# A fused attention and GEGLU block on one core: side matmuls paced by columns per iteration with fillers, two head quads interleaved, one gelu instruction in the last feed-forward group

## The chip, the core and the metric

The kernel runs on one core of one Trainium2 chip. A core has five engines that follow their own instruction lists and wait for each other by semaphores: PE (matmuls, from SBUF into the accumulation memory PSUM), ACT (one function per element, here mostly exp), DVE (other elementwise work), POOL, and SP, which here only issues DMAs. [...]

The metric is the device time of one execution in microseconds (us): the median of three runs. A separate execution was profiled; its trace is what the text reads.

## What is computed

One transformer block on 2048 tokens of width 512, with 32 heads of width 16 and a hidden width of 1792. Six modulation vectors come from a conditioning vector c.

```
mod = (silu(c) @ w_mod).reshape(1, 6, 1, -1)
sa, ca, ga, sb, cb, gb = mod[:, 0..5]
h = layernorm(x) * (1 + ca) + sa
q, k, v = heads of h @ wqkv
p = softmax(q @ k.T * 16**-0.5);  o = p @ v
x = x + ga * (o @ wo)
h = layernorm(x) * (1 + cb) + sb
x = x + gb * ((gelu(h @ w_gate) * (h @ w_up)) @ w_down)
```

gelu is the tanh form. Weights and activations are bfloat16, sums are float32.

## The kernel before, in words

**Blocks.** Queries are taken in five groups (`GROUPS`): three of 512 tokens, two of 256. Within a group the heads are taken in eight quads of four heads (`qd`), and the keys in 128-token tiles. A "tile" of scores is one head's 128 keys by 512 query columns (or two such key tiles by 256), one PSUM bank. There are 2048 such tiles.

**The main loop** (`stream`) runs 683 iterations. Iteration c takes the next three tiles: `qk` issues their score matmuls on PE into three of six PSUM banks (`scp`, shown as `ps_sc`; two sets of three alternate), and ACT makes one exp of 128 x 1536 into the SBUF ring `E` of 24 slots. Then PE multiplies earlier exp results with the values (`pv_round`: four matmuls that run side by side, one per head of the quad, into the bank `pv`), always two iterations behind. A column of ones in the values gives the softmax denominators; at the end of a quad DVE copies the bank to `osb`, and the denominators are turned into reciprocals by way of DRAM (`fin1`, `fin2`, put off by 5 and 10 iterations).

**Order on PE.** PE runs its list in order. The score matmuls of iteration c+1 wait for the exp of iteration c-1, since they write its banks, and the exp of c+1 waits for them. Whatever else stands in PE's list between two score groups delays the next score group, and so may delay ACT.

**Side work.** Everything else goes through the eighth bank, `mi` (`ps_mi`): the projections of q, k, v (`proj_q`, `proj_k`, `proj_v`; 4 matmuls of 512 columns, or 16 of 128), transposes (8 of 128 columns), the output projection (`wo`: 8 matmuls of 512 per 128 tokens) and the feed-forward part of the group before (`G`, `U`: 4 matmuls each; `down`: 14 per 128 tokens). `first_side` and `group_side` return lists of such items. Each item issues all its matmuls at once and then the DVE instruction that empties `mi`; `stream` spreads the items evenly over the iterations through the table `sched`. So an iteration has either no side matmul, or a whole item of 1024, 2048, 4096 or 7168 columns.

**First stage.** The prologue loads inputs, computes layernorm of tokens 0 to 511, and projects k and q of the first quad pair. Keys of the other three token groups (512 tokens each) are made inside the loop: layernorm statistics (`ln_stat`) and normalization on DVE, transposes and modulation, then K and V. Quad 0 walks over all 16 key tiles first, so its fifth iteration or so already needs the second token group, and so on.

**Gelu.** In the loop, gelu is made from DVE products and an ACT Tanh, so that exp and tanh share ACT's function table. The last group's feed-forward part (`tail`) does the same with ACT Square and Copy, five DVE instructions per pair of chunks and a Tanh, in a four-stage software pipeline.

**Queues.** The first loads are issued by SP and ACT; all later DMAs by SP.

## Time and profile before

| what | value |
|---|---|
| time, median of 3 runs | 1115.35 us (1114.75 to 1116.24) |
| the profiled execution | 1115.72 us |
| its span, first to last instruction | 1114.0 us |
| first exp starts, last exp ends | 18.7 us, 1069.2 us |
| exp instructions in the loop | 683 |
| mean granted PE clock | 0.779 |

The span divides into three parts: up to the first exp (lead), from there to the end of the last exp (stream), and the rest (tail). In the views that follow, a row of the timeline gives start, duration, engine, operation, the tile written and those read, a count, and in brackets how long the engine stood idle before it and what ended that. A row of the windows gives a stretch, the busy time in it and the granted PE clock as a share of full speed.

### The profile page before, as it was taken

What the parts mean: (1) busy time and instruction counts of PE and PEld (TensorE: products, weight loads), DVE (VectorE), ACT (ScalarE), POOL (GpSimd) and SP (SyncE); (2) the same over time, 40 slices, a digit from 0 to 9 for tenths busy, and PEclk for the clock granted to TensorE, in tenths of its full rate; (3) what the DMA queues carried; (4) which work ended last, traced back from release to release, by engine and by line L of the source; (5) the groups of instructions that cost most, each with busy time, mean ns of one, the idle gap of its engine ahead of it and who ended that gap; (6) DMA issues with size and microseconds to landing.
All of it is one profiled execution on the core that took longest, in us unless ns stands there. A gap on an engine that the chain in (4) does not pass through costs nothing.

```text
span 1114.0 us, 15292 instructions
## 1 busy us (share of the span) xinstructions
PE 853.9 (77%) x6638; PEld 257.9 (23%) x6638; DVE 362.9 (33%) x796; ACT 967.4 (87%) x740; POOL 7.2 (1%) x13
## 2 busy tenths in 40 slices
PE   5677777777777777777778788788787878787757
PEld 2222222211121111112212111112222223222225
DVE  7732223121033222321123322231126552343346
ACT  2489999999979999998799999999888997999924
POOL 2000000000000000000000000000000000000000
PEclk7688888787577777777967767776969999668878
DMA  6000000520000000000000000000000000000000
GB/s 246 1 1 11 11 11 11 183 55 11 11 1 11 10 11 11 11 9 7 25 11 11 11 11 11 11 1 11 29 12 12 11 12 25 9 13 9 11 15 10
DMA packets 28621, 24.97 MB, mean 22 GB/s; under 512 B 14445, under 2 KB 22826, under 8 KB 28554
## 3 DMA queue, kind: packets, MB, share of 16 engines
q1 hardware_dynamic: 27226, 22.16, 6.8%
q10 hardware_dynamic: 1328, 1.84, 0.5%
q8 instruction: 52, 0.85, 0.3%
q14 instruction: 15, 0.12, 0.0%
HBM read 21.36 MB, written 2.61 MB: 22 GB/s over the span
## 4 chain that ended last, share of the span: by engine, by line
ACT 64%; PE 29%; DVE 6%; issue 1%; DMA 0%; DVEq 0%
ACT E L210 62%; PE ps_mi L201 16%; PE ps_sc L201 9%; PE ps_pv L201 3%; ACT wreg L210 2%; DVE st L243 1%; PE ps_mi L205 1%; DVE nwt L213 1%; DVE hreg L220 1%; DVE xw L213 0%; DVE mv L246 0%; DVE rstd L224 0%; DVE xs L213 0%; DMA xs<-in_A_x_dram 0%; DVE kme L220 0%
## 5 line engine op out<-in xcount | busy, mean ns | idle before, releaser
L210 ACT ACTIVATE E<-ps_sc 128x1536 bf16<-128x1536 f32 (+2 forms) x697 | 939.8, 1485 | 107.0 <-PE ps_sc L201 106.3
L201 PE MATMUL ps_sc<-qT,kme 32*128 32x512 bf16 (+1 forms) x1280 | 171.4, 419 | 108.2 <-ACT E L210 105.8
L201 PE MATMUL ps_pv<-E,vaug 128*17 128x512 bf16 (+1 forms) x2560 | 244.4, 409 | 5.2 <-DVE osb L227 3.9
L201 PE MATMUL ps_sc<-qT,kmo 32*128 32x512 bf16 (+1 forms) x1280 | 164.4, 401 | 102.9 <-ACT E L210 101.7
L201 PE MATMUL ps_mi<-wreg,mreg 128*128 128x512 bf16 (+1 forms) x448 | 142.2, 455 | 1.2 <-DVE wreg L227 0.9
L201 PEld LDWEIGHTS ps_sc<-qT,kme 32*128 32x128 bf16 x1280 | 37.6, 96 | 245.9 <-ACT E L210 219.7
L201 PEld LDWEIGHTS ps_sc<-qT,kmo 32*128 32x128 bf16 x1280 | 37.3, 94 | 233.0 <-ACT E L210 198.3
L201 PEld LDWEIGHTS ps_pv<-E,vaug 128*17 128x17 bf16 x2560 | 52.1, 89 | 164.2 <-issue 150.0
L227 DVE CAST wreg<-ps_mi 128x512 bf16<-128x512 f32 (+1 forms) x56 | 35.0, 625 | 165.5 <-PE ps_mi L201 165.5
L213 DVE TENSOR_TENSOR hreg<-ps_mi,wreg 128x512 bf16<-128x512 f32 (+1 forms) x56 | 34.9, 623 | 97.6 <-PE ps_mi L201 97.3
L201 PEld LDWEIGHTS ps_mi<-wreg,mreg 128*128 128x128 bf16 x448 | 40.7, 112 | 68.5 <-issue 49.3
L201 PE MATMUL ps_mi<-dreg,hreg 128*128 128x512 bf16 x210 | 54.0, 402 | 0.1
L213 DVE TENSOR_TENSOR wreg<-wreg 128x1024 bf16<-128x1024 bf16 (+1 forms) x84 | 52.5, 626 | 2.9
L227 DVE COPY osb<-ps_pv 128x512 f32<-128x512 f32 (+1 forms) x40 | 23.3, 582 | 76.8 <-PE ps_pv L201 76.6
L201 PE MATMUL ps_mi<-hreg,wreg 128*128 128x512 bf16 x120 | 44.8, 513 | 0.0
L213 DVE TENSOR_TENSOR onorm<-osb,rb 128x512 bf16<-128x512 f32 (+1 forms) x40 | 23.2, 580 | 52.8 <-DMA rb<-scr_rec 52.8
L201 PE MATMUL ps_mi<-wo,onorm 128*128 128x512 bf16 x112 | 36.1, 480 | 0.2 <-DVE xw L213 0.2
L213 DVE TENSOR_TENSOR xw<-ps_mi,gb 128x512 bf16<-128x512 f32 x15 | 10.4, 692 | 67.7 <-PE ps_mi L201 67.6
L220 DVE TENSOR_SCALAR wreg<-wreg 128x1024 bf16<-128x1024 bf16 (+1 forms) x56 | 21.9, 392 | 30.2 <-ACT wreg L210 29.3
L220 DVE TENSOR_SCALAR kmo<-ps_mi,rm 128x512 bf16<-128x512 f32 x15 | 11.3, 750 | 55.3 <-PE ps_mi L201 55.3
L210 ACT ACTIVATE wreg<-wreg 128x1024 bf16<-128x1024 bf16 (+1 forms) x28 | 28.5, 1018 | 0.0
L227 DVE CAST qT<-ps_mi 128x512 bf16<-128x512 f32 x15 | 10.4, 692 | 51.8 <-PE ps_mi L201 51.8
(94 smaller groups left out, 343.5 us busy)
## 6 DMA issues: line engine op xcount, KB each, us to landing
rb<-scr_rec SPq DMA_DIRECT2D x96, 64.0 KB, 2.0
mreg<-in_w_mod_dram SPq DMA_DIRECT2D x1, 2048.0 KB, 17.6
out_dram<-xs SPq DMA_DIRECT2D x16, 128.0 KB, 1.7
rb<-scr_rec SPq DMA_DIRECT2D x60, 32.0 KB, 1.8
mreg<-in_B_w_gate_dram SPq DMA_DIRECT2D x1, 1792.0 KB, 7.2
mreg<-in_B_w_up_dram SPq DMA_DIRECT2D x1, 1792.0 KB, 11.3
dreg<-in_B_w_down_dram SPq DMA_DIRECT2D x1, 1792.0 KB, 17.2
wreg<-in_A_wqkv_dram SPq DMA_DIRECT2D x1, 1536.0 KB, 10.6
```

The costliest lines, as they stand in the source:

```text
L201: return self.rec("pe", lambda e: e.matmul(out, lhsT, rhs, start=start, stop=stop, tile_position=tp), [lhsT, rhs], [out])
L205: return self.rec("pe", lambda e: e.transpose(out, in_, ident), [in_, ident], [out])
L210: return self.rec("act", lambda e: e.activation(out, in_, func, scale=scale, **kw), rd, [out])
L213: return self.rec(eng, lambda e: e.tensor_tensor(out, a, b, op), [a, b], [out])
L220: return self.rec(eng, lambda e: e.tensor_scalar(out, a, s1, s2, **kw), rd, [out])
L227: return self.rec(eng, lambda e: e.tensor_copy(out, in_), [in_], [out])
L243: return self.rec("dve", lambda e: e.bn_stats(out, in_), [in_], [out])
```

## The change

The diff has four parts.

**1. Side work as generators, paced.** `first_side` and `group_side` become generators (`side_first`, `side_k`, `side_v`, `side_q`, `side_mod`, `side_wo`, `side_ffn`) that yield before each piece of up to 512 columns, -1 (or -2, -4) where the next piece must wait for one (two, four) iterations because DVE has to empty `mi`, and 0 at the end. `plan` gives each generator a first and a last iteration; `pump` hands out columns per iteration so that the work left is spread over the iterations left. `require` runs a generator forward at once where a key or value tile is needed that isn't made yet. Where an iteration has under `FILL` = 1280 columns in all (counted with 128 for each score tile and 512 for each `pv_round`) and `mi` is free, `stream` adds filler matmuls into `mi` whose result nobody reads.

**2. First two quads interleaved.** The first 128 tiles go by token group: group 0 of quad 0 and quad 1, group 1 of both, and so on. Quad 1 accumulates in the sixth bank of `scp`, so these 140 tiles (128 and a run-out of 12) go in chunks of three and two in turn: 56 exps for 140 tiles, and 692 exps in all. `osb`, `rb` and their DRAM copies get two to four slots by size, and the 256-column groups use separate columns of `onorm` (`OCOL`), so that `wo` of one group may lie later.

**3. Prologue.** The first loads are ordered anew and `wqkv` comes in six pieces; silu of c is made in columns (`tcol`) from four one-column matmuls, before the statistics on DVE; statistics of token tiles 4 to 8 move to ACT (Copy and Square with accumulated sums, two instructions a tile); more warm-up matmuls stand between.

**4. Tail.** The denominators' selection matmul (`self32`) goes ahead of the `wo` matmuls; the feed-forward part uses one `Gelu_apprx_tanh` per pair of chunks on ACT, one DVE instruction for the product with `up`, and a two-stage order.

```diff
+FILL = 1280
+OCOL = (0, 0, 0, 0, 256)
...
+    def require(self, keys):
+        for key in keys:
+            while key not in self.have:
+                w = self.work[0]
+                w[4] = next(w[0], 0)
...
+    def side_proj(self, col, g, fin):
+        mi = self.mi[:, :]
+        for dci in range(NDC):
+            yield 512
+            self.mm(mi, self.wqkv[:, dci, col:col + P], self.hT[:, dci, 512 * g:512 * g + 512],
+                    start=(dci == 0), stop=(dci == NDC - 1))
+        fin(mi)
+        yield -1
...
+    def plan(self, gstart):
+        a = gstart[1]
+        w = [(self.side_first, 0, 30)]
+        w.append((lambda: self.side_dc(1), 30, 51))
...
+        for gi in range(len(GROUPS) - 1):
+            last = gi == len(GROUPS) - 2
+            s0 = gstart[gi + 1] + 11
+            w.append((lambda gi=gi: self.side_wo(gi), s0, s0 + 5 * GROUPS[gi][1] // P))
+            w.append((lambda gi=gi: self.side_ffn(gi), s0, gstart[gi + 2] + (-3 if last else 10)))
...
+    def pump(self, it):
+        used = 0
+        while self.work:
+            gen, s, e, left, pend = self.work[0]
+            if it < s:
+                break
+            if used == 0 and not self.pumped:
+                rate = left / max(1, e - it)
+                self.credit = min(self.credit + rate, max(1536, 2 * rate))
+                self.pumped = True
...
+            if it < self.free_at or self.credit < pend / 2:
+                break
+            self.credit -= pend
+            used += pend
...
+            n = min(2 if b < nsplit + 12 and len(chunks) % 2 else CH, len(seq) - b)
...
-            for f in sched.pop(c, []):
-                f()
+            if c < nit:
+                cols += self.pump(c)
+                debt = min(1536, max(0, debt + FILL - cols))
+                if self.free_at <= c and not self.open:
+                    while debt >= 512:
+                        self.mm(self.mi[:, :], self.ident[:, :], self.E[:, 0, :])
+                        debt -= 512
...
+        self.act_stat(8)
+        self.act_stat_fin(4, 8)
...
-            self.act(wb[p], bk, ACT.Square)
-            self.act(gb[p], bk, ACT.Copy)
-            self.ts(dve, wb[p], wb[p], GELU_C, 1.0, ALU.mult, ALU.add)
-            self.tt(dve, wb[p], wb[p], gb[p], ALU.mult)
+            self.act(self.E[:, ci, 0:m], bk[:, 0:m], ACT.Gelu_apprx_tanh, scale=1.0)
```

How it moves PE's list shows at two places. The rows name the tile written, then those read: `ps_sc<-qT,kme` are score matmuls of an even quad (`kmo`: odd), `ps_pv<-E,vaug` the products with the values, `ps_mi` side work.

PE before, from the first score group of the loop on (V of group 0, then both transposes of group 1, then K of group 1):

```order
L201 MATMUL ps_sc<-qT,kme 128x512 x3
L201 MATMUL ps_mi<-wreg,hreg 128x128 x16
L201 MATMUL ps_sc<-qT,kme 128x512 x3
L205 MATMUL ps_mi<-ident,dreg 128x128 x8
L201 MATMUL ps_sc<-qT,kme 128x512 x3
L205 MATMUL ps_mi<-ident,dreg 128x128 x8
L201 MATMUL ps_sc<-qT,kme 128x512 x3
L201 MATMUL ps_pv<-E,vaug 17x512 x4
L201 MATMUL ps_mi<-hreg,wreg 128x512 x4
```

PE of the change at the same place:

```order
L205 MATMUL ps_sc<-qT,kme 128x512 x3
L205 MATMUL ps_mi<-wreg,hreg 128x128 x4
L205 MATMUL ps_sc<-qT,kme 128x512 x2
L205 MATMUL ps_mi<-wreg,hreg 128x128 x8
L205 MATMUL ps_sc<-qT,kme 128x512 x3
L205 MATMUL ps_mi<-wreg,hreg 128x128 x4
L205 MATMUL ps_sc<-qT,kme 128x512 x2
L205 MATMUL ps_pv<-E,vaug 17x512 x4
L209 MATMUL ps_mi<-ident,dreg 128x128 x4
L205 MATMUL ps_sc<-qT,kme 128x512 x3
L205 MATMUL ps_pv<-E,vaug 17x512 x4
L209 MATMUL ps_mi<-ident,dreg 128x128 x4
```

The score groups hold three and two tiles in turn, V of group 0 is spread over three iterations, and four score groups instead of two stand ahead of the first transposes of group 1.

PE before, in the feed-forward part of group 0, where the down projection of 128 tokens is one item:

```order
L201 MATMUL ps_sc<-qT,kmo 128x512 x6
L201 MATMUL ps_pv<-E,vaug 17x512 x4
L201 MATMUL ps_mi<-dreg,hreg 128x512 x14
L201 MATMUL ps_sc<-qT,kmo 128x512 x3
L201 MATMUL ps_pv<-E,vaug 17x512 x4
```

PE of the change in the same down projection:

```order
L205 MATMUL ps_sc<-qT,kme 128x512 x3
L205 MATMUL ps_pv<-E,vaug 17x512 x4
L205 MATMUL ps_mi<-dreg,hreg 128x512
L205 MATMUL ps_sc<-qT,kme 128x512 x3
L205 MATMUL ps_mi<-dreg,hreg 128x512
L205 MATMUL ps_sc<-qT,kme 128x512 x3
L205 MATMUL ps_pv<-E,vaug 17x512 x4
L205 MATMUL ps_mi<-dreg,hreg 128x512 x2
```

The 14 matmuls are dealt out one or two to an iteration. Over the whole list the change has 40 filler matmuls (`ps_mi<-E,ident`), 25 of them between iterations 134 and 215, where the q projections of the later groups run out.

More of the change, by code (lines that the diff above doesn't have):

```diff
@@ L553, in first_side @@
[L553 to L561 removed]
+            self.ts("dve", dst[:, :], mi, s, None, ALU.mult)
+            yield -1
+        yield 512
@@ L563, in ln2 @@
+        yield -1
     def ln2(self, tiles):
@@ L591, in group_side @@
         mi = self.mi[:, :]
-        items = []
-        def wo(i):
-            self.wo_mm(mi, i, range(8))
+        while gi not in self.onorm_done and not self.dry:
+            yield -1
+        for i in range(n):
+            for qd in range(8):
+                yield 512
+                self.wo_mm(mi, gi, i, qd)
             self.wo_fin(mi, tiles[i])
@@ L647, in group_side @@
-        for i in range(n):
-            items.append(lambda i=i: down(i))
-        return items
+            yield -1
     def later(self, d, fn):
-        self.defer.append((self.it + d, fn))
+        if not self.dry:
+            self.defer.append((self.it + d, fn))
     def flush(self, force=False):
@@ new lines, in stream @@
+            for qd in range(first, 8):
+                for r in range(n):
+                    add(gi, qd, r)
+        chunks = []
+        self.slot = []
+        e = b = 0
+        while b < len(seq):
+            n = min(2 if b < nsplit + 12 and len(chunks) % 2 else CH, len(seq) - b)
+            if e + n > NSL:
+                e = 0
+            chunks.append((b, n, CH * (len(chunks) % 2), e))
+            self.slot += [e + i for i in range(n)]
+            b, e = b + n, e + n
+        cof = {b + i: c for c, (b, n, _, _) in enumerate(chunks) for i in range(n)}
@@ L776, in tail @@
     def tail(self, gi):
-        self.flush(True)
+        for _ in range(1):
+            self.flush(True)
+        while self.work:
+            for _ in self.work.pop(0)[0]:
+                pass
+            self.flush(True)
         act, dve = "act", "dve"
@@ L849, in tail @@
+        for s in range(len(chunks) + 1):
+            if s < len(chunks):
+                G(s)
+                U(s)
+            if s >= 1:
+                dn(s - 1)
         for i in range(n):
```

588 lines of the change are left out of this document (363 added, 225 removed).

## The prediction, as it was put on record

> **What bounds the kernel now.** First the page, with the shares of the engines:
>
> ```profile
> PE 853.9 (77%) x6638; PEld 257.9 (23%) x6638; DVE 362.9 (33%) x796; ACT 967.4 (87%) x740; POOL 7.2 (1%) x13
> ```
>
> and the chain that ended last:
>
> ```profile
> ACT 64%; PE 29%; DVE 6%; issue 1%; DMA 0%; DVEq 0%
> ```
>
> ACT is busy for 87% and holds 64% of the chain; PE holds most of the rest, although PE isn't full. So ACT sets the pace and PE sometimes makes it wait. The view of waits says how often:
>
> ```profile
> ACT E L210 <- PE ps_sc L201: 106.3, 90, 6.0
> ```
>
> 106.3 us in 90 waits for scores. Next, where: ACT's busy time by stretches, from the first exp (18.7 us) to the end of the last one (1069.2 us). Columns: stretch, its length, busy time and count, granted PE clock, DMA share, GB/s.
>
> ```profile
> 18.70:65.00 46.30, 19.60 (x14) 0.67 0.03 12
> 65.00:305.00 240.00, 228.80 (x170) 0.80 0.12 36
> 305.00:348.00 43.00, 34.73 (x27) 0.74 0.03 7
> 348.00:522.00 174.00, 162.14 (x122) 0.75 0.03 9
> 522.00:550.00 28.00, 18.39 (x15) 0.89 0.09 25
> 550.00:776.00 226.00, 219.38 (x165) 0.71 0.04 10
> 776.00:860.00 84.00, 72.11 (x54) 0.84 0.07 18
> 860.00:916.00 56.00, 56.00 (x44) 1.00 0.04 10
> 916.00:1069.20 153.20, 139.32 (x108) 0.79 0.06 15
> ```
>
> Length minus busy time, summed, is 100.0 us idle in a stream of 1050.5 us (the rest of the 106.3 lies in the tail). I sort it by what stands in PE's list there: the **first stage** 26.7 us; the three stretches of ordinary 2048-column items (65 to 305, 348 to 522, 550 to 776) 11.2 + 11.9 + 6.6 = 29.7 us; and the four with `wo` or `down` items (305 to 348, 522 to 550, 776 to 860, 916 on) 8.3 + 9.6 + 11.9 + 13.9 = 43.7 us. The stretch from 860 to 916 has side work too, and no idle time: there the clock is 1.00.
>
> Why the clock decides, in PE's timeline: an item at full clock,
>
> ```profile
> 68.67 0.39 PE L201 MATMUL ps_pv<-E,vaug 128*17 128x512 bf16 x4
> 68.99 1.04 PE L201 MATMUL ps_mi<-hreg,wreg 128*128 128x512 bf16 x4
> 69.96 0.39 PE L201 MATMUL ps_sc<-qT,kme 32*128 32x512 bf16 x3
> ```
>
> and the same at half clock.
>
> ```profile
> 77.75 0.59 PE L201 MATMUL ps_sc<-qT,kmo 32*128 32x512 bf16 x3 [0.63 <-ACT E L210]
> 78.27 0.61 PE L201 MATMUL ps_pv<-E,vaug 128*17 128x512 bf16 x4
> 78.81 1.89 PE L201 MATMUL ps_mi<-hreg,wreg 128*128 128x512 bf16 x4
> 80.63 0.61 PE L201 MATMUL ps_sc<-qT,kmo 32*128 32x512 bf16 x3
> ```
>
> From start to start, `pv` takes 0.32 us and the item 0.97 at full clock; 0.54 and 1.82 at half, where the score group takes 0.52. ACT runs through the first without a gap:
>
> ```profile
> 66.83 13.55 ACT L210 ACTIVATE E<-ps_sc 128x1536 bf16<-128x1536 f32 x10
> ```
>
> and waits after the second:
>
> ```profile
> 81.28 9.51 ACT L210 ACTIVATE E<-ps_sc 128x1536 bf16<-128x1536 f32 x7 [0.90 <-PE ps_sc L201]
> ```
>
> The wait is 0.90. A lone exp takes 1.45, so the pitch is (13.55 - 1.45) / 9 = 1.344 us, and each restart costs 1.45 - 1.344 = 0.106 more.
>
> What sets the clock, in PE's busy time in stretches of 3.41 us (the clock changes only on such a grid in this trace):
>
> ```profile
> 258.76:262.18 3.42, 1.49 (x17) 0.99 0.00 0
> 262.18:265.59 3.41, 3.41 (x18) 0.51 0.03 5
> 265.59:269.00 3.41, 2.71 (x25) 1.00 0.00 0
> 859.51:862.92 3.41, 2.15 (x24) 1.00 0.00 1
> 862.92:866.34 3.42, 2.71 (x39) 1.00 0.04 6
> ```
>
> At full clock a stretch that was busy for 1.49 (44%) is followed by half clock; one of 2.15 (63%) or more stays full. At half clock a stretch that was busy throughout is followed by full. So the gaps between items let the clock fall, and the next item meets it at half.
>
> **The change part by part.**
>
> *Ordinary items dealt out.* By PE's list a usual iteration gets 512 or 1024 side columns, on average 1.17 matmuls of 512. At full clock PE then needs 0.32 (scores) + 0.75 x 0.32 (`pv` comes in three of four iterations) + 1.17 x 0.97 / 4 = 0.84 of 1.344 us. Without side work the stretch at 258.76 was busy for 44%; 1.17 x 0.24 / 1.344 = 21% come on top: 65%, just above the 63% that stayed full. When the clock does fall, PE needs 0.52 + 0.75 x 0.54 + 1.17 x 1.82 / 4 = 1.46 us, more than 1.344, so it is busy throughout and should be back a stretch later. One such stretch holds 2.5 iterations and loses 2.5 x 0.12 = 0.3 us, less than the lead that PE has: scores may be begun 1.344 before they are needed and take 0.52. Of 29.7 us I leave 3; bounds 0 and 10 (none, or a third of today's). The 40 fillers take 40 x 0.24 = 10 us of PE time in idle iterations; nothing waits for them but the next score group.
>
> *`wo` and `down` items.* Four `down` items between 522 and 550 cost 9.6, 2.4 each; now their 14 matmuls go one to three an iteration. This removes most of 43.7. New is a **dense place**: the feed-forward part of group 2 (512 tokens) must end within the 85 iterations of a 256-token group, and by PE's list gets 1493 side columns an iteration, 2.9 matmuls, for some 50 iterations: 0.32 + 0.24 + 2.9 x 0.24 = 1.26 of 1.344 us at full clock. The old list had 1194 there (860 to 916, no idle time). Each group of four must also wait until DVE has emptied `mi`, 0.63 us by this group of the page (mean in ns):
>
> ```profile
> L227 DVE CAST wreg<-ps_mi 128x512 bf16<-128x512 f32 (+1 forms) x56 | 35.0, 625 | 165.5 <-PE ps_mi L201 165.5
> ```
>
> Scores and `pv` of the next iteration (0.64) cover it only where no other DVE work stands ahead; I let 0.2 show per iteration, so that PE falls behind by 0.1: 5 us in 50. The four `wo` places with layernorm behind them keep 5 in all (8.3 at the first today). Together 10 of 43.7 stay; bounds 4 and 25.
>
> *First stage.* The long waits come once for each token group. ACT's timeline has this one:
>
> ```profile
> 42.26 1.45 ACT L210 ACTIVATE E<-ps_sc 128x1536 bf16<-128x1536 f32 x1 [4.82 <-PE ps_sc L201]
> ```
>
> and a token group later this:
>
> ```profile
> 57.02 1.45 ACT L210 ACTIVATE E<-ps_sc 128x1536 bf16<-128x1536 f32 x1 [5.86 <-PE ps_sc L201]
> ```
>
> A token group takes 14.8 us (57.02 - 42.26) to be normalized, transposed and projected; one quad gives 16 tiles, 5.3 exps, 7.2 us of ACT work for it. With two quads it is 32 tiles, 14.3 us: nearly equal. Besides, the statistics now run between the other steps. What stays: the first `pv` still waits for DVE (normalization of group 1, then V), about 2.5 us more than the first four exps cover; and 56 iterations in which PE is full, with K's two DVE instructions (twice the 0.63 above) before the next group, some 0.13 an iteration. Of 26.7 I leave 10; bounds 5 and 18. Next late there is the DVE that empties `mi`.
>
> *More exps.* The chunks of two make 692 exps of 683. A 1024 exp saves only its columns, so each further one costs its fixed part, about 0.1 (its 512 columns are about 0.4 of 1.344, three of which leave 0.1): 1.0 us.
>
> *Restarts.* With some 65 of 90 waits gone, 65 x 0.106 = 6.9 us less.
>
> *Lead.* ACT takes two more DMA issues and eight statistics instructions ahead of its first work:
>
> ```profile
> 13.76 1.63 ACT L210 ACTIVATE hreg<-ps_sc,modA 128x512 bf16<-128x512 bf16 x2 [9.51 <-PE ps_sc L205]
> ```
>
> and two for tile 8 ahead of the first exp:
>
> ```profile
> 18.70 1.45 ACT L210 ACTIVATE E<-ps_sc 128x1536 bf16<-128x1536 f32 x1 [0.58 <-PE ps_sc L201]
> ```
>
> Eight of about 0.8 (half of 1.63) fit into the 9.51 that ACT waits, with three to spare for the DMA issues; the two for tile 8 take 1.6 where 0.58 was idle: +1.0. Against it silu in columns takes two instructions on a row of 512 and one wait for PE off DVE's path, about as much: 0. Bounds -2 and +2, since the loads are queued anew (six DMAs for `wqkv`, SP's `w_mod` part behind two others).
>
> *Tail.* PE does 14 of the 16 `wo` matmuls first,
>
> ```profile
> 1069.75 5.53 PE L201 MATMUL ps_sc<-wo,onorm 128*128 128x512 bf16 x14
> ```
>
> and the last two after the selection, the reciprocal and a product on DVE:
>
> ```profile
> 1078.02 1.03 PE L201 MATMUL ps_sc<-wo,onorm 128*128 128x512 bf16 x2 [2.31 <-DVE onorm L213]
> ```
>
> With the selection first, the 2.31 of reciprocal and product lie beside the 14 matmuls: -2. In the feed-forward part PE has the same 112 + 28 matmuls. The 112 run like this now (shortest, median and longest in ns, first and last start),
>
> ```profile
> L201 PE MATMUL ps_sc<-wreg,mreg x112: 272/273/421, 1087.1 to 1107.5; 128*128 128x256 bf16 x112
> ```
>
> and the 28 have this pitch at full clock:
>
> ```profile
> 1095.83 0.38 PE L201 MATMUL ps_mi<-dreg,hreg 128*128 128x512 bf16 x1
> 1096.05 0.38 PE L201 MATMUL ps_pv<-dreg,hreg 128*128 128x512 bf16 x1
> ```
>
> That is 0.22 for 512 columns and 0.11 for 256: 112 x 0.11 + 24 x 0.22 = 17.6 from the first start to where the last four down matmuls begin, against 20.7 today (1107.5 - 1087.1 and 0.3 of that matmul); 1.4 given back for a cold start: -1.7. Tail 44.8 - 3.7 = 41.1; bounds 38 and 46. The gelu needs another function table; this trace has one such load, 1.28 us at the start, and the first two groups of matmuls cover it. [...] No row here shows a switch.
>
> **Sum.** Stream: 1050.5 - (29.7 - 3) - (43.7 - 10) - (26.7 - 10) + 1.0 - 6.9 = 967.5. Span 18.7 + 967.5 + 41.1 = 1027.3. The profiled execution took 1115.72 for 1114.0, so 1.7 lie outside: **1029 us**. Its time is 0.4 above the median of 1115.35, which I neglect.
>
> **The rivals.**
>
> *Hand-offs at `mi` take the place of the bursts.* Every group ends with DVE emptying the one bank, and the next begins one iteration later instead of two or three. For: in the dense place and the first stage PE has under 0.1 us to spare. Against: elsewhere it has 0.5. If the dense place loses 0.3 an iteration (15 instead of 5) and the first stage 18, the time is 1029 + 10 + 8 = 1047.
>
> *The clock doesn't follow the density.* The stretch at 258.76 fell to half while PE was busy for 1.49 us of it. [...] As a mechanism of this kernel: if the share of full clock stays as it is (0.78 on average), about 44% of the stretches are at half; spells of two or more lose 0.3 to 1 us beyond the lead, some 40 of them 15 us: 1044.
>
> *The first stage isn't shortened*, because layernorm on DVE sets its pace with two quads as with one: 26.7 stay, 1046.
>
> *Slower than before: PE stays at half clock.* If 65% busy is too little to keep full clock and busy at half doesn't bring it back, each iteration costs 1.46 us, with hand-offs 1.55: 692 x 1.55 = 1073, with lead, tail and 1.7 outside 1134. It decides from 1.52 us an iteration, (1115.7 - 61.5) / 692. Against: 262.18 to 265.59 came back.
>
> **How the numbers follow.** Forecast (1010 to 1040, likeliest 1029): 0.64. Hand-offs 1047: 0.13. Clock not following 1044: 0.07. First stage 1046: 0.07. Everything at its lower bound, under 1010: 0.05. Slower, at half clock: 0.03, and 0.01 that this just balances. The unknown costs, each at its bound, move the sum by -20 to +35 together, seldom all one way; the range 1008 to 1052 takes in all rivals but the slow one. About 0.2% is what a measurement of this kernel can tell from no change. Faster 0.96, same 0.01, slower 0.03.
>
> **What would show it.** ACT's waits for scores fall from 106 us to about 30, in under 40 waits; the stretch of the first 56 exps has about 10 us idle; the granted clock of the stream rises above 0.9; no side group of 14 in the timeline; the tail is 41 us. It is wrong if the clock stays near 0.78, if PE in the dense place is late in every iteration, or if ACT waits for the table load.

## The result, and the profile after

The changed kernel takes 1078.37 us (median; 1067.60 to 1094.47), the kernel before 1115.36: a ratio of 0.964, 95% interval 0.956 to 0.971. It is faster by 37 us, where 86 were forecast. Its single runs spread far more than those of before, and go with the granted PE clock: spans of 1065.8 us at 0.835, 1074.6 at 0.820, 1092.7 at 0.778. The ratio and its interval leave out the run of 1094.47, a slow one (the 0.778). The profiled execution took 1076.38 us.

From the page of the changed kernel: the engines' busy time, the chain that ended last, and the granted clock in 40 slices.

```profile
PE 883.6 (82%) x6685; PEld 249.7 (23%) x6685; DVE 348.1 (32%) x749; ACT 974.5 (91%) x756; POOL 7.2 (1%) x13
...
ACT 55%; PE 34%; DVE 9%; issue 1%; DMA 0%; DVEq 0%; ACTq 0%
...
PEclk9557998757778855779998879589998899969998
```

ACT's share of the chain fell, from 64% to 55%, and PE's rose from 29% to 34%. PE is busy 30 us longer than before, although its useful work hardly changed. That isn't more time at half clock: split by the trace's clock, its busy time at half fell from 433 to 362 us and at full rose from 416 to 517. The side work now comes in more and smaller groups, and each group has a price of its own, read below; how much of the 30 us that makes was not separated. Slices of five in the clock row, some in a line, show where the clock was low. ACT's wait for scores in the view of waits (total us, count, longest), which stood at 106.3 us in 90 waits:

```profile
ACT E L218 <- PE ps_sc L205: 70.4, 121, 2.0
```

A third of the time is gone; the waits are more and shorter (forecast: 30 us in under 40). To compare stages I cut both traces at the same work: the ends of the exps that finish 140 tiles (the stage with two quads interleaved), then query groups 0, 1, 2, 3 and 4. Columns: stretch, length, busy time and count of PE, PEld, DVE, ACT and POOL, granted clock, DMA share, GB/s. Before:

```profile
18.70:112.80 94.10, 63.60 (x489) 24.39 (x488) 43.21 (x115) 64.89 (x48) 0.00 (x0) 0.76 0.03 9
112.80:289.40 176.60, 132.34 (x996) 38.97 (x996) 36.55 (x62) 167.91 (x126) 0.00 (x0) 0.81 0.15 45
289.40:558.00 268.60, 203.43 (x1241) 51.70 (x1241) 69.17 (x132) 238.86 (x180) 0.00 (x0) 0.75 0.04 11
558.00:806.90 248.90, 202.30 (x1241) 50.60 (x1241) 69.30 (x132) 237.25 (x179) 0.00 (x0) 0.73 0.05 12
806.90:944.80 137.90, 110.57 (x1240) 36.31 (x1240) 64.16 (x132) 123.29 (x95) 0.00 (x0) 0.90 0.06 15
944.80:1069.20 124.40, 99.38 (x1180) 32.83 (x1180) 42.11 (x118) 118.28 (x93) 0.00 (x0) 0.76 0.05 13
```

After:

```profile
18.56:112.40 93.84, 80.43 (x485) 26.64 (x483) 40.67 (x108) 67.17 (x58) 0.00 (x0) 0.62 0.05 17
112.40:289.50 177.10, 144.57 (x1008) 39.46 (x1007) 34.60 (x56) 168.93 (x126) 0.00 (x0) 0.81 0.16 45
289.50:539.10 249.60, 213.14 (x1246) 48.29 (x1246) 69.49 (x132) 240.20 (x179) 0.00 (x0) 0.76 0.04 12
539.10:782.30 243.20, 198.63 (x1251) 47.77 (x1251) 69.16 (x132) 238.58 (x180) 0.00 (x0) 0.84 0.04 12
782.30:915.10 132.80, 109.14 (x1223) 32.98 (x1222) 61.97 (x130) 123.64 (x94) 0.00 (x0) 0.93 0.05 13
915.10:1035.20 120.10, 97.46 (x1212) 31.86 (x1209) 42.62 (x110) 118.31 (x93) 0.00 (x0) 0.91 0.06 17
```

The first 140 tiles are not shorter at all (94.10 and 93.84), and the clock there fell from 0.76 to 0.62. Of the stream's gain of 33.9 us, 33.6 lie behind them. The clock is above 0.9 only in the last two stages.

What such a spell looks like: four neighbouring stretches of 3.41 us in a spell at half clock from 373 to 441 us.

```profile
380.46:383.87 3.41, 3.41 (x21) 0.60 (x17) 0.00 (x0) 2.97 (x3) 0.00 (x0) 0.50 0.00 0
383.87:387.29 3.42, 3.10 (x19) 0.56 (x16) 2.71 (x5) 3.17 (x3) 0.00 (x0) 0.50 0.01 2
387.29:390.70 3.41, 3.41 (x21) 0.65 (x17) 0.95 (x2) 3.41 (x4) 0.00 (x0) 0.50 0.02 2
390.70:394.11 3.41, 3.41 (x17) 0.62 (x13) 1.32 (x4) 3.24 (x4) 0.00 (x0) 0.50 0.03 2
```

PE is busy throughout in three of them, and the clock stays at half behind each. Counted over the stream (stretches at half clock with PE busy for over 98% by its records): before the change 49 of 52 were followed by full clock, now 28 of 70. PE's timeline in that spell:

```profile
389.06 1.04 PE L205 MATMUL ps_mi<-wreg,mreg 128*128 128x512 bf16 x2
390.03 0.61 PE L205 MATMUL ps_sc<-qT,kmo 32*128 32x512 bf16 x3
390.57 0.61 PE L205 MATMUL ps_pv<-E,vaug 128*17 128x512 bf16 x4
391.11 0.61 PE L205 MATMUL ps_mi<-wreg,mreg 128*128 128x512 bf16 x1
391.65 0.61 PE L205 MATMUL ps_sc<-qT,kmo 32*128 32x512 bf16 x3
```

Two side matmuls take 0.97 from start to start of what follows, one takes 0.54: a matmul behind another of its group adds 0.43, a new group costs 0.11 more. At the pitch of 0.43 for 512 columns, 0.11 of a lone matmul's 0.54 streams nothing (an estimate from these rows), but the records, which overlap, show PE as busy. So pieces of one matmul stream at most 512 x 3.41 / 0.54 = 3230 columns in a stretch at half clock, and an item of four as before the change (1.82 us, in the prediction's rows) 2048 x 3.41 / 1.82 = 3840. ACT, for its part, waits at nearly every exp:

```profile
392.30 4.15 ACT L218 ACTIVATE E<-ps_sc 128x1536 bf16<-128x1536 f32 x3 [0.17 <-PE ps_sc L205]
396.62 1.45 ACT L218 ACTIVATE E<-ps_sc 128x1536 bf16<-128x1536 f32 x1 [0.17 <-PE ps_sc L205]
398.67 1.45 ACT L218 ACTIVATE E<-ps_sc 128x1536 bf16<-128x1536 f32 x1 [0.60 <-PE ps_sc L205]
```

Spells at half clock became fewer and longer: 64 of 2.2 stretches on average, the longest 37.5 us, before; 28 of 3.9 now, the longest 71.7 us, in the first stage.

**Theory.** In this kernel the clock goes by the columns that PE streams in a stretch of 3.41 us. In the traces of before and of the change, full clock stayed behind 257 of 257 stretches with over 3400 columns and behind 3 of 89 with under 3200; half clock ended behind 72 of 76 with over 3400 and behind none of 106 with under 3200 (the last section has the count). The change's floor of 1280 columns an iteration is 1280 x 3.413 / 1.344 = 3251 at ACT's pace in the floor's own count, which has 384 for three tiles of scores where the count of the stretches has 512: little margin or none. And stretches of single pieces at half clock, by the estimate above 3230 at most, seldom get back. **Rivals:** DVE's chain and the hand-offs at `mi` cost the time whatever the clock; the used area of the array or unbroken runs set the clock, not columns.

### The profile page after: what moved, and what is told of

Read it like the earlier page. It is cut to its first block, busy times and chain, and to the rows that moved or that the text cites. A ratio compares the mean times of both kernels' runs of the same rounds, so it can differ in the third digit from the quotient of the medians.

```text
span 1074.6 us, 15365 instructions
## 1 busy us (share of the span) xinstructions
PE 883.6 (82%) x6685; PEld 249.7 (23%) x6685; DVE 348.1 (32%) x749; ACT 974.5 (91%) x756; POOL 7.2 (1%) x13
## 4 chain that ended last, share of the span: by engine, by line
ACT 55%; PE 34%; DVE 9%; issue 1%; DMA 0%; DVEq 0%; ACTq 0%
ACT E L218 54%; PE ps_mi L205 14%; PE ps_sc L205 12%; PE ps_pv L205 7%; ACT wreg L218 1%; PE ps_mi L209 1%; DVE wreg L235 1%; DVE wreg L221 1%; DVE kme L228 1%; DVE hreg L221 1%; DVE kmo L228 1%; DVE nwt L221 1%; DVE wreg L228 1%; DVE hreg L228 0%; DVE st L251 0%
## 5 line engine op out<-in xcount | busy, mean ns | idle before, releaser
L205 PE MATMUL ps_pv<-E,vaug 128*17 128x512 bf16 (+1 forms) x2496 | 228.2, 392 | 5.2 <-DVE osb L235 2.5
L205 PE MATMUL ps_sc<-qT,kme 32*128 32x512 bf16 (+1 forms) x1280 | 168.6, 400 | 64.8 <-ACT E L218 61.1
L205 PE MATMUL ps_mi<-wreg,mreg 128*128 128x512 bf16 (+1 forms) x448 | 159.5, 427 | 15.9 <-DVE hreg L221 9.3
L205 PE MATMUL ps_mi<-dreg,hreg 128*128 128x512 bf16 x210 | 72.9, 399 | 0.9 <-DVE xw L221 0.5
L235 DVE CAST wreg<-ps_mi 128x512 bf16<-128x512 f32 x49 | 33.8, 691 | 114.6 <-PE ps_mi L205 114.5
L205 PEld LDWEIGHTS ps_mi<-wreg,mreg 128*128 128x128 bf16 x448 | 37.6, 101 | 107.2 <-issue 55.7
L221 DVE TENSOR_TENSOR hreg<-ps_mi,wreg 128x512 bf16<-128x512 f32 x49 | 33.6, 686 | 83.4 <-PE ps_mi L205 83.3
L205 PE MATMUL ps_mi<-hreg,wreg 128*128 128x512 bf16 x120 | 55.1, 496 | 2.2 <-DVE vaug L235 1.0
L205 PE MATMUL ps_mi<-wreg,hreg 128*128 128x128 bf16 x256 | 27.4, 258 | 8.7 <-DVE kmo L228 8.7
L235 DVE CAST qT<-ps_mi 128x512 bf16<-128x512 f32 x15 | 10.4, 691 | 74.4 <-PE ps_mi L205 74.4
L221 DVE TENSOR_TENSOR xw<-ps_mi,ga 128x512 bf16<-128x512 f32 x14 | 9.7, 691 | 57.6 <-PE ps_mi L205 57.6
## 6 DMA issues: line engine op xcount, KB each, us to landing
mreg<-in_w_mod_dram SPq DMA_DIRECT2D x1, 2048.0 KB, 14.5
```

Source lines behind the costliest of these rows:

```text
L205: return self.rec("pe", lambda e: e.matmul(out, lhsT, rhs, start=start, stop=stop, tile_position=tp), [lhsT, rhs], [out])
L221: return self.rec(eng, lambda e: e.tensor_tensor(out, a, b, op), [a, b], [out])
L235: return self.rec(eng, lambda e: e.tensor_copy(out, in_), [in_], [out])
```

## The experiments

### Floors, pacing and order one at a time

**Warm start.** 17 matmuls of zeros where PE idles ahead of the first `pv`:

```diff
+            if rp == 0:
+                for _ in range({0: 3, 1: 4, 2: 4, 3: 6}.get(c, 0)):
+                    self.mm(self.pv[:, :], self.warm[:, 0:P], self.warm)
```

> The changed kernel with 17 extra matmuls of zeros (128x512, into the still empty ps_pv) laid behind the score groups of the first four iterations, where PE waits for ACT and DVE; nothing else moves. In the profiled run of the changed kernel the clock fell at 21.6 us and stayed at half until 93.3 us; the first 140 score tiles took 93.8 us from the first exp (94.1 before the change), where ACT alone needs about 65. Theory (the clock follows the number of columns that PE streams in a stretch of 3.41 us, and once it is at half, PE itself is the bound and cannot stream enough to get back): the stage starts at full clock and stays there, the 140 tiles take 72 to 80 us, the time is 1052 to 1066. Rival (DVE's chain of layernorm, transposes, modulation and K sets the pace of the first stage): 90 to 95 us as now, time within 6 of 1078.

Measured: 1086.92 us (1072.43 to 1091.32), no gain; the first 140 tiles took 89.0 us. The theory's 72 to 80 missed, and the rival's 90 to 95 came closer. The stage did start at full clock, and lost it here (windows, then PE's timeline, of this run; quad 1's products with the values go into `ps_sc`):

```profile
31.81:35.23 3.42, 2.96 (x32) 1.38 (x32) 1.08 (x3) 2.96 (x3) 0.00 (x0) 1.00 0.01 2
35.23:38.64 3.41, 1.58 (x12) 0.50 (x12) 3.03 (x17) 3.41 (x4) 0.00 (x0) 1.00 0.02 5
38.64:42.05 3.41, 2.82 (x19) 1.50 (x19) 2.25 (x6) 1.36 (x2) 0.00 (x0) 0.50 0.00 0
```

```profile
36.77 0.39 PE L205 MATMUL ps_sc<-qT,kme 32*128 32x512 bf16 x3 [0.96 <-ACT E L218]
37.09 0.39 PE L205 MATMUL ps_sc<-E,vaug 128*17 128x512 bf16 x4
37.98 1.68 PE L209 MATMUL ps_mi<-ident,dreg 128*128 128x128 bf16 x8 [0.49 <-DVE dreg L228]
```

While DVE normalizes the next token group (`-2` in the generator) PE has no side work, 1.58 us busy in the stretch, and the clock falls; it stays at half for 48 us. So the fall of the clock fits the theory, but a start alone doesn't carry it over the stage's own holes.

**A higher floor.** 1664 columns, with fillers also inside open groups of `mi`, which add zero:

```diff
-FILL = 1280
+FILL = 1664
...
+                elif self.open and self.region is not None:
+                    out = self.region
+                    n = out.shape[-1]
+                    while debt >= 512:
+                        self.mm(out, self.zero[:, 0:P], self.qT[:, 0, 0:n], start=False, stop=False)
+                        debt -= n
```

> The changed kernel with a floor of 1664 columns an iteration instead of 1280, and with fillers that may also stand inside an open accumulation in ps_mi (a matmul with a weight tile of zeros that adds nothing): 282 small fillers inside groups, 50 between them. By the order of PE's list 4% of the stretches of 3.41 us then hold under 3400 columns at ACT's pace, against 31% in the changed kernel. Theory (columns per stretch set the clock, about 3400 of them): mean granted clock over 0.93, ACT's waits for scores under 30 us, time 1010 to 1035. Rival A (DVE's hand-offs at ps_mi cost the time, whatever the clock): clock up, time still above 1060. Rival B (the clock does not follow columns but something else, such as long runs without a change of tile): clock near 0.82, and 0.2 us more PE time in the iterations at half, 1090 to 1120.

Measured: 1043.49 us (1043.02 to 1047.68), ratio 0.936 (0.933 to 0.940), clock 0.941. Both rivals fall: some 300 more matmuls that compute nothing take 35 us off the time. The size fell short of the theory's 1010 to 1035: ACT still waits 50.1 us for scores, where under 30 were expected, and the first 140 tiles still took 88.1 us.

**Whole groups again.**

```diff
-            if it < self.free_at or self.credit < pend / 2:
+            if it < self.free_at or (not self.open and self.credit < pend / 2):
```

> The changed kernel with the pacing taken out: a side group, once begun, is issued whole (4 matmuls of 512 for most, 8 for wo, 14 for down), as before the change; the new order of the first stage, the fillers (432 now, since the debt grows between groups), the prologue and the tail stay. Theory (what the gaps cost is the clock; bursts bring the clock back within a stretch): 21% of stretches hold under 3400 columns, no spell at half clock longer than 15 us outside the first stage, time 1045 to 1075. Rival (the step in the prediction that counted bursts as the cause of ACT's waits, at whatever clock): 1090 to 1110, with waits of 0.9 us behind each group.

Measured: 1235.58 us (1232.75 to 1236.62), outside of both. The number of fillers rose to 432, and they wait for something new, in the view of waits:

```profile
PE ps_mi L205 <- ACT E L218: 125.7, 58, 3.0
```

The change's fillers read the first slot of `E`; where that slot is being written, PE, in order, stops behind the filler until the exp is done. The run says nothing on pacing.

**Quads in turn.**

```diff
-                for g in range(4):
-                    for qd in range(2):
-                        for r in range(4):
-                            add(gi, qd, 4 * g + r)
+                for qd in range(2):
+                    for r in range(16):
+                        add(gi, qd, r)
```

> The changed kernel with the first two head quads one behind the other again (all 16 key tiles of quad 0, then quad 1), all else as changed. The prediction had counted 16.7 us for the interleaving. If it brings that, the first 140 tiles take 105 to 115 us and the time is 1090 to 1098. Theory (the first stage is set by PE at half clock, not by the order of the quads): the 140 tiles take 90 to 100 us, time 1072 to 1086.

Measured: 1083.71 us (1070.75 to 1093.92); 94.0 us for the first 140 tiles, both as the theory had them. As the change stands, interleaving brings nothing that can be told.

### Fillers that wait for nobody, on both kernels

The fillers move to `ps_pv`, which stays open over a whole quad, with 17 columns of zeros as weights; the change's own are taken out (first kernel, which has the warm start too). The same goes into the kernel before, without anything else of the change (second).

```diff
+FLOOR = 1664
...
+                self.debt = min(1536, max(0, self.debt + FLOOR - self.cn))
+                self.cn = 0
+                while self.debt >= 512 and self.pvopen:
+                    out, w = self.pvopen
+                    self.mm(out, self.zero[:, 0:VW], self.qT[:, 0, 0:w], start=False, stop=False, tp=(0, 0))
+                    self.cn = 0
+                    self.debt -= w
```

> The changed kernel with its own fillers taken out, a floor of 1664 columns an iteration by fillers in the open accumulation of the values' product instead (ps_pv: 17 columns of zeros as weights, 512 columns streamed, some 360 of them; no DVE reads that bank in between, and they may stand in the pauses of the first stage too), and the 17 matmuls of zeros in the first four iterations. Theory (columns streamed per stretch of 3.41 us set the clock, whatever part of the array they use): clock over 0.96, the first 140 tiles in 72 to 80 us (88.1 with the floor inside ps_mi, 93.8 in the changed kernel), time 1022 to 1036. Rival A (the used area of the array counts, and 17 of 128 columns are little): clock near 0.82, time 1070 to 1100. Rival B (DVE's chain sets the first stage even at full clock): 140 tiles still 85 or more, time 1036 to 1045.

> The kernel before the change with nothing but a floor of 1664 columns an iteration by fillers of zeros in the open accumulation of ps_pv (some 540). Items stay whole, quads in turn, old prologue and tail. Theory (the bursts cost ACT's waits because they met half clock): clock over 0.93 outside the first stage, time 1048 to 1070. Rival (a burst delays the next scores at any clock, so pacing is needed): clock up, but ACT's waits stay over 80 us and the time over 1095. If the clock counts the used area of the array, neither changes.

Measured: on the change 1036.48 us (1032.75 to 1040.29), clock 0.970; on the kernel before 1067.71 (1067.02 to 1068.30), clock 0.968. The clocks and the second time came as the theory had them. The first kernel's time lies just over the theory's range and within that of rival B (DVE's chain), and its first stage took 84.7 us, not 72 to 80:

```profile
19.07:103.80 84.73, 72.10 (x529) 26.48 (x534) 40.24 (x108) 66.47 (x58) 0.00 (x0) 0.88 0.05 16
```

So far DVE's chain is not ruled out there. **Fillers alone, on the old kernel with its bursts, bring 48 us, more than the whole change.** There the view of waits and two timelines read:

```profile
ACT E L218 <- PE ps_sc L207: 67.0, 46, 6.0
```

```profile
617.99 1.04 PE L207 MATMUL ps_mi<-wreg,mreg 128*128 128x512 bf16 x4
619.01 0.39 PE L207 MATMUL ps_sc<-qT,kmo 32*128 32x512 bf16 x3
619.33 0.39 PE L207 MATMUL ps_pv<-E,vaug 128*17 128x512 bf16 x4
619.55 0.38 PE L207 MATMUL ps_pv<-qT,zero 128*17 128x512 bf16 x1
```

```profile
601.02 21.96 ACT L218 ACTIVATE E<-ps_sc 128x1536 bf16<-128x1536 f32 x16
```

Whole items of four stand between the scores, and ACT makes 16 exps without a gap: at full clock a burst fits into the lead. That 17 of 128 columns of the array do as well as 128 (0.970 against 0.941 for the floor in `mi`) takes the rival of the used area away.

**Pacing undone, and fillers taken out.** The first has the edit of whole groups and `FILL = 0`, the second `FILL = 0` alone.

> The changed kernel with the pacing undone alone: a side group, once begun, is issued whole, and there are no fillers (the 432 of the run before this waited for ACT's exps, whose first tile they read). The rest of the change stays. What it is slower than 1078 is what the pacing is worth. The prediction's sum gave the pacing 60 us of the stream and 7 of restarts: 1130 to 1145. Theory (pacing trades bursts, which bring the clock back at once, for spells at half clock, and keeps less than half of that gain): 1095 to 1115, with a clock near 0.78 and no spell at half over 20 us outside the first stage.

> The changed kernel without its 40 fillers, pacing kept. Theory: by the order of PE's list 35% of the stretches then hold under 3400 columns instead of 31%; a little more time at half clock between iterations 134 and 215, 1080 to 1095. Rival (fillers do nothing for the clock): within 4 of 1078.

Measured: without pacing 1122.20 us (1115.16 to 1124.14), 7 us more than before the change, outside both ranges. Without fillers 1072.38 (1068.58 to 1093.17), within 6 of the change and under the theory's 1080 to 1095, which missed: its 40 fillers do nothing that can be told. These two kernels differ by the pacing alone, so pacing is worth 50 us, less than the prediction's 67 and more than the theory allowed. The surprise is the first stage without pacing:

```profile
18.93:93.30 74.37, 56.29 (x471) 22.40 (x476) 40.73 (x108) 64.53 (x59) 0.00 (x0) 0.89 0.06 19
```

74.4 us with the same 40.7 us of DVE work, where the paced stage took 93.8, and without fillers this:

```profile
19.00:111.00 92.00, 74.95 (x477) 25.83 (x482) 40.67 (x108) 67.14 (x58) 0.00 (x0) 0.65 0.04 15
```

DVE's work alone doesn't set these 92 to 94 us.

### Where pacing hurts, and how much floor is needed

Four kernels, compared on one chip. The first three issue groups whole: in the first 50 iterations on top of the floor, everywhere on top of the floor, and in the first 50 iterations of the change as it is. The edit is that of the first and third; the second has it without `it < 50`. The fourth has the floor at 1280.

```diff
-            if it < self.free_at or self.credit < pend / 2:
+            if it < self.free_at or (not (self.open and it < 50) and self.credit < pend / 2):
```

> The kernel with the floor of 1664 in ps_pv and the 17 matmuls at the start (1036.48 us), and besides side groups issued whole in the first 50 iterations, paced behind them. In the run without pacing the first 140 tiles took 74.4 us, with pacing 93.8, with pacing and floor 84.7. Theory (in the first stage each group is a link of a chain through DVE, and dealing its matmuls out over two or three iterations makes the chain longer): 140 tiles in 70 to 76 us, time 1022 to 1029, faster than every kernel so far. Rival (the 74.4 came only from that run's clock of 0.89 there): 82 to 87 us, 1033 to 1040.

> The floor of 1664 in ps_pv with side groups issued whole throughout, no pacing anywhere (some 800 matmuls' worth of fillers, since whole groups leave empty iterations between). It shows what pacing is worth while the clock is full. Theory (a burst of 4 matmuls at full clock, 0.97 us, fits into the lead; only groups of 8 and 14 stop ACT): first 140 tiles as in the run before, after them 10 to 25 us more than with pacing (891.6 us with the floor and pacing), time 1035 to 1055. Rival (bursts cost the same at any clock): the 44 us by which the kernel without pacing is slower stay, time over 1070.

> The changed kernel with side groups issued whole in its first 50 iterations, and nothing else (no floor, no matmuls at the start, the fillers as they are). If the pacing itself lengthens the first stage: 140 tiles in 72 to 80 us instead of 93.8, time 1056 to 1070. If only the clock does, and it stays at half as now: 90 us or more, 1072 to 1086.

> As the kernel with the floor of 1664 in ps_pv, but with the floor at 1280, the number that the change uses (82 fillers instead of 454). At ACT's pace 1280 columns an iteration are 1280 x 3.413 / 1.344 = 3251 in a stretch, where the traces so far show a fall in nearly every stretch under 3200 and hardly one over 3600. Theory: the clock falls as often as in the changed kernel, mean 0.80 to 0.86, time 1058 to 1080. Rival (the place of the fillers did it, not their number): clock over 0.93, time under 1045.

Measured, in this order: 1030.03 us (1029.24 to 1031.43), the fastest; 1049.67 (1045.83 to 1052.39); 1072.30 (1068.90 to 1083.46); 1063.54 (1055.35 to 1067.60) with clocks of 0.83 to 0.87. The first, second and fourth came out as the theory had them; the first's time lies 1 us over its range, and its 76.2 us for the first 140 tiles just over 70 to 76. The third missed: its first stage took 89.4 us and its time is at the edge of its rival's 1072 to 1086, but at a clock of 0.85 there and not at half. Its PE timeline shows a cause:

```profile
23.18 0.63 PE L205 MATMUL ps_mi<-E,ident 128*128 128x512 bf16 x1 [4.02 <-DVE vaug L235]
```

A filler right behind the V group waits for DVE to empty `mi`, and PE stands for 4.02 us with scores behind it. In this first stage the trace has 24 fillers, and PE's waits at `mi` for DVE sum to 14.5 us in the view of waits. So the last two runs: that kernel without fillers, and a floor between the two tried.

> The changed kernel with side groups whole in the first 50 iterations and without fillers. With the fillers in ps_mi that kernel took 89.4 us for the first 140 tiles; there PE stood 4.02 us behind a filler that waited for DVE to empty ps_mi. If the fillers there were the cause: 140 tiles in 74 to 80 us, time 1052 to 1066. If pacing behind the first stage or the clock alone decides, 88 us or more, 1068 to 1084.

> As the kernels with the floor in ps_pv at 1664 (1036.48 us) and at 1280 (1063.54 us), at 1472 (234 fillers; 1472 x 3.413 / 1.344 = 3738 columns in a stretch at ACT's pace, just over the 3600 from which the traces show no fall). Theory (a bound near 3400 to 3600 columns): clock over 0.94, time 1034 to 1044. Rival (the more filler the better, no bound): halfway between the two, 1047 to 1053.

Measured: 1058.31 us (1053.57 to 1063.22), first 140 tiles

```profile
18.44:92.90 74.46, 58.73 (x477) 22.19 (x474) 39.93 (x107) 64.45 (x57) 0.00 (x0) 0.85 0.06 22
```

as expected of the fillers; the same waits sum to 4.1 us. The floor of 1472 gave 1054.92, with runs of 1038.92 (clock 0.947), 1052.43 (0.916), 1057.41 (0.910) and 1060.80 (0.904): one within the theory's range, one within its rival's, two over both. The times don't decide between them. That 3738 at ACT's pace leaves too little for the stretches in which PE waits is likely, not shown; with the floor of 1664 in `pv` the four runs had clocks of 0.965 to 0.976.

The fastest kernel, chain and waits and the same stages as above:

```profile
ACT 77%; PE 14%; DVE 8%; issue 1%; DMA 0%; DVEq 0%; ACTq 0%
```

```profile
ACT E L224 <- PE ps_sc L209: 33.9, 53, 2.0
```

```profile
18.47:94.70 76.23, 68.83 (x539) 25.37 (x544) 39.38 (x107) 65.24 (x58) 0.00 (x0) 0.94 0.06 21
94.70:263.40 168.70, 141.67 (x1085) 43.86 (x1100) 35.78 (x58) 166.88 (x126) 0.00 (x0) 0.99 0.16 47
263.40:501.80 238.40, 196.88 (x1319) 53.60 (x1343) 69.52 (x132) 236.75 (x180) 0.00 (x0) 0.97 0.04 12
501.80:740.50 238.70, 198.69 (x1324) 53.73 (x1348) 69.24 (x132) 236.87 (x179) 0.00 (x0) 0.96 0.05 13
740.50:869.00 128.50, 102.70 (x1238) 34.74 (x1259) 62.11 (x130) 123.52 (x94) 0.00 (x0) 1.00 0.06 14
869.00:987.50 118.50, 98.11 (x1263) 35.65 (x1270) 42.54 (x109) 118.07 (x92) 0.00 (x0) 0.99 0.07 17
```

All runs side by side, the stages from the same cuts of each trace, the clock of the profiled run. Without a high floor the profiled run can lie far off the median (1072.43 for the warm start, 1070.75 for quads in turn), so small differences between stages there mean nothing. The kernel before took 1113.6 to 1115.5 us beside each set of runs.

| kernel | first 140 tiles, us | rest of the exps, us | clock | median, us |
|---|---|---|---|---|
| before | 94.1 | 956.4 | 0.779 | 1115.36 |
| changed | 93.8 | 922.8 | 0.820 | 1078.37 |
| changed, quads in turn | 94.0 | 917.2 | 0.854 | 1083.71 |
| changed, warm start | 89.0 | 923.4 | 0.823 | 1086.92 |
| changed, no fillers | 92.0 | 916.6 | 0.790 | 1072.38 |
| changed, groups whole, no fillers | 74.4 | 982.0 | 0.773 | 1122.20 |
| changed, groups whole, fillers in `mi` | 88.6 | 1086.0 | 0.818 | 1235.58 |
| changed, groups whole at first | 89.4 | 922.5 | 0.842 | 1072.30 |
| the same, no fillers | 74.5 | 919.4 | 0.816 | 1058.31 |
| floor 1664 in `mi` | 88.1 | 900.8 | 0.941 | 1043.49 |
| floor 1280 in `pv` | 92.5 | 910.1 | 0.865 | 1063.54 |
| floor 1472 in `pv` | 89.4 | 910.0 | 0.910 | 1054.92 |
| floor 1664 in `pv` | 84.7 | 891.6 | 0.970 | 1036.48 |
| the same, groups whole at first | 76.2 | 892.8 | 0.971 | 1030.03 |
| the same, groups whole throughout | 74.0 | 911.5 | 0.988 | 1049.67 |
| before, floor 1664 in `pv` | 92.8 | 912.6 | 0.968 | 1067.71 |

## Why the prediction was wrong

The direction was right, and the forecast missed by 47 us in the profiled run (1076.38 against 1029). Cut at the same places: lead 18.56 (18.7 forecast), stream 1016.6 (967.5), tail 1074.6 - 1035.2 = 39.4 (41.1). All of it is in the stream: 16.4 us in the first stage (-0.3 instead of -16.7) and 32.7 behind it (-33.6 instead of -26.7 - 33.7 - 6.9 + 1.0 = -66.3). Split the other way, ACT's idle time in the stream fell from 100.0 to 59.8 us, where 23 were to stay, and its busy time rose by 6.4 (950.5 to 956.8), where the terms for more exps and restarts had -5.9: the waits became 121 instead of some 25, and each is a restart.

*"Busy throughout and should be back a stretch later": the step that failed.* It was read off one pair of stretches, in which a whole item ran. Busy in the records is not the same as streaming: with single pieces a stretch at half clock can be busy to the full and hold no more than 3230 columns (the estimate above). Of 70 stretches at half clock that were busy throughout, 42 were not followed by full clock. An iteration at half clock then costs ACT 0.17 to 0.6 of waiting each time, where the prediction let a single stretch of 2.5 iterations lose 0.3, inside the lead. Holding the clock with the floor of 1664 and leaving the rest of the change brings the rest of the stream from 922.8 to 891.6, and against before's 956.4 that is -64.8, where the sum had -66.3. ACT is then idle for 9.9 us behind the first stage (13 forecast). So the terms for ordinary and `wo`/`down` items were sized well for full clock, and the clock was not there.

*"65% just above the 63% that stayed full."* The mean may have been right; the margin was none. By the order of PE's list (an estimate made before the experiments), 31% of the stretches at ACT's pace hold under 3400 columns, and each can start a spell by the theory; in the trace 28 of 187 stretches at full clock did.

*The bursts as the cause of ACT's waits.* Only in part. With the clock held, the old kernel's bursts lose 912.6 - 891.6 = 21 us against pacing and all else of the change, and whole groups throughout 911.5 - 892.8 = 19. The other 44 us that the old kernel lost behind the first stage were the clock at which the bursts ran (956.4 - 912.6). Without a floor pacing is worth 50 us in the median, and 65 behind the first stage (982.0 - 916.6); but that kernel places its whole groups by credit rather than evenly and is 26 us slower there than the kernel before, which was not separated further.

*First stage, 10 us left of 26.7.* In the cut at 140 tiles ACT was idle for 94.10 - 64.89 = 29.2 us before, and for 93.84 - 67.17 = 26.7 now. The prediction dealt with the order of the quads and with DVE, and let a full PE and the hand-offs cost 0.13 an iteration. Two things stand in its place. The clock was at half for 71.7 us. And pacing makes each group a longer link of the chain: without fillers the stage took 92.0 us paced (clock 0.65) and 74.5 whole (0.85); with the floor, 84.7 paced (0.88) and 76.2 whole (0.94). The paced stage at a clock of 0.88 is still 10 us longer than the whole one at 0.85, so the clock is only a part of it.

*"Nothing waits for them but the next score group"* left out that a filler itself waits: for DVE to empty `mi`, or for the exp that writes the tile it reads. In the changed kernel's first stage that cost nothing that can be told (its trace has one filler there). Once groups are whole, 24 stand there, and the stage takes 89.4 us with them and 74.5 without. So issuing groups whole helps only where the fillers leave `mi`. Whether interleaving the quads pays then was not tried; with pacing it doesn't.

*Rivals.* "The first stage isn't shortened" came true as to its size, not as to its reason (layernorm on DVE): DVE did the same 40 us of work in 74.4 us. "PE stays at half clock", with 0.03 the least likely, happened in spells (1.59 us an iteration in the rows of ACT above, (398.67 - 392.30) / 4; it had named 1.46 to 1.55); it wasn't the whole stream, hence faster and not slower. "Hand-offs" came true in part, as the longer chain of the paced first stage. In the dense place (query group 3) ACT is idle for 132.80 - 123.64 = 9.2 us; in the fastest kernel, at a clock of 1.00, for 5.0, the 5 of the forecast. "The clock doesn't follow the density" is refuted: the floors of 1280, 1472 and 1664 gave clocks of 0.865, 0.910 and 0.970. PE's busy time alone does not tell: with the warm start the clock fell behind a stretch in which PE was busy for 1.58 of 3.41 us, and behind 42 stretches of the change that were busy throughout it stayed at half.

*Right:* the lead and the tail as sums, and the table load. In the tail (ACT, then PE):

```profile
1050.49 1.28 ACT L218 ACT_TABLE_LOAD   x1
1052.35 0.60 ACT L218 ACTIVATE E<-ps_sc 128x512 bf16<-128x512 f32 x1 [0.58 <-PE ps_sc L205]
```

```profile
1050.07 5.20 PE L205 MATMUL ps_sc<-wreg,mreg 128*128 128x256 bf16 x32 [0.23 <-ACT wreg L218]
```

The load takes 1.28 and lies beside PE's first matmuls; ACT still waits 0.58 for them behind it. From the end of ACT's instruction before it (1050.47) to the start of the next it is 1.88 in all, the 0.58 included.

The fastest kernel's stream takes 969.0 us with 21.7 idle, and its profiled run 1029.38, where the sum had 967.5, 23 and 1029. That the whole comes out so closely is partly luck: its first stage has whole groups, which the forecast did not have in mind.

## What to carry to other kernels

Before spreading a burst of matmuls, read from the trace how the granted clock goes with what PE streams in a stretch, and count what the spread leaves in each; here the spread traded short spells at half clock for longer ones (2.2 stretches on average before, 3.9 after). Fillers belong where they wait for nobody and nobody waits for them (zeros into an accumulation that is open anyway, reading a constant tile), with a margin for the holes: here a floor of 1664 held the clock at 0.970 where 1472 gave 0.910. In this first stage, a chain through DVE, it paid to issue each link whole (76.2 us instead of 84.7, with the floor).

## What the runs showed of the hardware

Stretches of 3.41 us within the exps, 307 in the trace of before and 297 in that of the change, by the columns that PE streamed in a stretch, and what the clock was in the next. The columns are laid out from the start of each matmul record at 0.22 us for 512 (0.43 at half clock); tiles that run side by side, up to four, count once.

```
columns        at full clock: stayed     at half clock: came back
under 3200       3 of   89                  0 of  106
3200 to 3400     6 of   12                 19 of   64
over 3400      257 of  257                 72 of   76
```

These are counts from one run of each kernel; a rule behind them was not shown. Near 3400 the count is blurred: some matmul records are missing, and the edges of stretches are known only as well as the trace shows them. The floors count 384 for three tiles of scores where this table has 512, so a floor of 1280 stands for up to (1280 + 128) x 3.413 / 1.344 = 3576 columns here, at ACT's pace.

With floors of 1280, 1472 and 1664 in `pv` the profiled runs had clocks of 0.865, 0.910 and 0.970. The floor of 1664 in `mi`, with 128 columns of weights instead of 17, had 0.941.
